# The last item's products with W1-W2 by a seven-product scheme, with partial sums chained in one PSUM tile, and a new list of steps

## The chip, the cores and the metric

The kernel runs on one core of a Trainium2 chip. The metric is device time in microseconds (us) of one launch. In the profile, PE is TensorE's matmul, PEld its weight load, DVE is VectorE, ACT is ScalarE, POOL is GpSimd and SP is SyncE.

## The reference, cut to what matters

There are four batch items (B = 4), each with 8 heads, 768 positions and head size 64. A block-sorting attention gives each item a matrix X of 768 tokens by 512 channels. Then a feed-forward part follows:

```
h1 = x @ w1                 # 512 -> 1024
h2 = x @ w2                 # 512 -> 1024
out = maximum(h1, h2) @ w_out   # 1024 -> 512
```

The kernel uses that maximum(h1, h2) = h2 + relu(h1 - h2). So it forms D = W1 - W2 once, computes g = relu(X D), and then out = g W_out + X Wc with Wc = W2 W_out, which is also formed once. Inputs are loaded as bf16; PSUM and the outputs are fp32.

## The kernel before, in words

All of the kernel is one hand-written list of steps, the string `plan`. A step is a word such as `h3.0.1A`: a kind, its indices, and an engine letter at the end (A for ACT, D for DVE, P for POOL) that says who reads the result out of PSUM or does the sum. `token` calls one function for each word, and each engine executes its instructions in the order in which the words stand. PSUM is one pool of four tiles of two banks each (`psum`, tag "ps"), so at most four results wait for their readers at a time.

The front of the list prepares everything: `k`, `q`, `b` and `t` sort and turn K, Q and V, `s` and `v` are scores and values of the attention, `x` transposes its result into `xT`, `T` transposes W2 into `w2T`, `d` subtracts W2 from W1 in place (`w_difference`, after which `w1_sb` holds D), `c` forms Wc, `w` forms sums of weight blocks. The words `lk`, `lq`, `lf`, `lv` issue loads on POOL's queue. Item 0's work is mixed into this front; the items then overlap, and the last item (3) ends the list.

For each item, a step `h<item>.<ch>.<t>` (`moe_h`, line 719) computes g for one half `ch` of the tokens (384) and one of four pieces `t` of 256 features: eight matmuls of 384 columns at line 711 and one reader (ACT, line 725, or DVE, line 727). An item has eight such steps.

The output product of an item is done in two groups, `P` (token tiles 0 and 1 of each half) and `U` (tile 2), by `Group`. A group has seven steps, `P3.0` to `P3.6`, by a Strassen scheme: matrices are cut into 2 by 2 blocks, and seven block products with sums of blocks take the place of eight. The sums of X's blocks are `X` steps (`x_sums`, into `sums_x`), those of g's blocks `G` steps (`g_sums`), those of weights `w` steps. A product of `P` is 12 matmuls of 256 columns, one of `U` is 6 (line 839). Each product is read out of PSUM by a copy or an add (lines 865, 872, 874), and the add's other input is an earlier result in SBUF. The finished halves are stored by `store`, from SP's queue and, for the very last part, from ACT's.

After the item's transposes, the end of the list before is the eight `h3` steps, and then the fourteen steps of `P3` and `U3`, mixed with X and G sums.

Of the kernel before, what the change touches and what calls it, by code (L numbers as in the profile page):

```python
# [10 lines left out]
FP32 = mybir.dt.float32  # L11
BF16 = mybir.dt.bfloat16
# [4 lines left out]
def kernel(  # L17
# [16 lines left out]
    nc = tc.nc  # L34
# [16 lines left out]
    TCH = S // 2  # L51
# [15 lines left out]
    def ps_f32(name):  # L67
        return psum.tile([128, 1024], FP32, tag="ps", name=name)
# [663 lines left out]

    sums_g = big.tile([128, 3, 4, TCH], BF16, tag="sums_g", name="sums_g")
    sums_x = big.tile([128, 4, 2, TCH], BF16, tag="sums_x", name="sums_x")
    wt_early = big.tile([128, 2, 4, NW], BF16, tag="wt_early", name="wt_early")
    w2T_flat = w2T.rearrange("p f d -> p (f d)")
    wt_late = w2T_flat[:, 0 : 8 * NW].rearrange("p (n k f) -> p n k f", n=2, k=4)
# [72 lines left out]
    class Group:  # L810
# [66 lines left out]
        def store(self, ch, c0=0, c1=DMODEL, queue=nc.sync):  # L877
# [5 lines left out]
                in_=self.o[ch][:, :, c0:c1],  # L883
            )

        def step(self, at, eng):
            a = self.by_tile(self.a) if at else None
            if at == 0:
                n = len(self.tiles)
                self.ps = ps_f32("out_ps")  # L890
                self.a = opool.tile([128, self.w], FP32, tag=f"a{n}", name="a", bufs=1)
                if n == 1:
                    o = opool.tile([128, 2, DMODEL], FP32, tag="o1", name="o", bufs=1)
                    self.o = [o[:, ch : ch + 1] for ch in range(2)]
                    self.both = o
                else:
                    self.o = [
                        opool.tile([128, n, DMODEL], FP32, tag=f"o{n}", name="o", bufs=2)
                        for _ in range(2)
                    ]  # L900
                self.product(0, "a11", "b11", True)
                self.first = self.copy(self.by_tile(self.a), 0, eng)
            elif at == 1:
                self.product(1, 2, 2, True)
                self.second = self.add(1, 0, 1, a, [self.first], eng)
            elif at == 2:
                self.product(0, "a12", "b21", False)
                self.copy(self.part(0, 0), 0, eng)
            elif at == 3:
                self.product(1, 1, 1, False)  # L910
                self.third = self.add(0, 1, 1, a, [self.first], eng)
            elif at == 4:
                self.product(0, 3, 3, True)
                self.fourth = self.add(1, 1, 0, self.part(0, 1), [self.third], eng)
                if self.b == B - 1:
                    self.store(1, NW)
            elif at == 5:
                self.product(1, 4, "b22", False)
                self.fifth = self.add(0, 1, 1, a, [self.first, self.fourth], eng)
                if len(self.tiles) > 1 or self.b == B - 1:  # L920
                    self.store(0)
            else:
                self.product(0, "a22", 4, False)
                self.add(
                    1, 0, 0, self.part(1, 0), [self.first, self.second, self.fifth], eng, True
                )
                if self.b == B - 1:
                    self.store(1, 0, NW, nc.scalar)
                elif len(self.tiles) > 1:
# [44 lines left out]
    def token(text):  # L974
# [6 lines left out]
        if kind == "k":  # L981
            sort_k(*n, eng=eng)
        elif kind == "q":
            q_transposes(*n, eng)
        elif kind == "F":
            fills[0] = n[0] * 128
        elif kind == "s":
            scores(*n, fills.pop(0, 0))
        elif kind == "v":
            values(*n, fills.pop(0, 0))  # L990
        elif kind == "x":
            x_transposes(*n, eng)
        elif kind == "t":
            turn_v(slice(0, 128), eng, n[1] * 24, n[1] * 24 + 24)
        elif kind == "b":
            {0: sort_v, 2: sort_v_pair, 3: sort_v_halved}[n[0]](*n, eng=eng)
        elif kind == "p":
            pair_q(*n, eng)
        elif kind == "y":
            nc.gpsimd.tensor_copy(  # L1000
                out=landed.rearrange("p (c h n) -> p c h n", c=2, n=1),
                in_=xT[:, n[0] % 2, :, :, 0, 0:1],
            )
            nc.gpsimd.tensor_copy(out=landed[:, 0:2], in_=qT[n[0] + 1][:, 0:HP:2, 0, 0])
        elif kind == "lv":
            load_v(3, half=n[0])
        elif kind == "lk":
            load_k(n[0])
        elif kind == "lq":
            load_q(n[0])  # L1010
        elif kind == "w":
            weight_sums(*n, engine)
        elif kind == "c":
            w_product(n[0], eng)
        elif kind == "X":
            x_sums(*n, engine)
        elif kind == "G":
            g_sums(*n, engine)
        elif kind == "h":
            moe_h(*n, eng=eng)  # L1020
        elif kind == "ha":
# [17 lines left out]
    groups, fills = {}, {}  # L1039
    landed = const.tile([128, 4], BF16, tag="landed", name="landed")  # L1040
    plan = [
        """
        k0.1A d0P k0.2A b0.1A b0.3D q0.0D b0.0D b0.2A q0.1D s0.5 s0.4 v0.5 s0.6 T0D s0.7 v0.4
        s0.0 v0.6 s0.1 s0.2 v0.7 s0.3 x0.2D v0.2 x0.3A lk1 lq1 v0.1 ha0.1.0 v0.0 hb0.1.0A T3D
        T2A lf3 d1P x0.0A v0.3 ha0.1.1 lf2 d3D lf1 hb0.1.1A B0 T1A ha0.0.1 d2D x0.1A X0.1D
        ha0.1.3 lf0 hb0.1.3A ha0.0.0 ha0.0.2 hb0.0.2D ha0.1.2 hb0.0.0D w0.3D c3D X0.2D G0.1.1D
        w0.1D hb0.1.2A hb0.0.1D G0.0.1D k1.1D lq2 c0A G0.1.2D c2A X0.3D k1.2D G0.1.3D k1.0A
        X0.4D q1.0D G0.0.2D q1.1A c1D s1.1 t1.2D s1.6 w1.1D t1.3D ha0.0.3 w1.2D w0.2D t1.1D
        t1.0D hb0.0.3A lk2 s1.3 s1.7 w1.4D lk3 P0.0A G0.0.4D s1.2 w0.4D s1.4 P0.1D b2.3A G0.0.3D
        b2.1A p2.0D p2.1D G0.1.4D P0.2A w1.3D b2.6D b2.4A b2.0A P0.3D b2.5A b2.2D b2.7A q2.0  # L1050
        P0.4D v1.1 v1.7 s1.5 q2.1 P0.5D v1.4 v1.6 P0.6D x1.3 k2.2A s1.0 U0.0A v1.5 U0.1D v1.2
        x1.2 v1.0 U0.2A k2.1A v1.3 U0.3D k3.2D k2.0A U0.4D U0.5D x1.0 x1.1 s2.7 s2.5 s2.6 U0.6D
        h1.1.0A v2.5 h1.1.3A X1.1D v2.7 X1.2D X1.4D k3.1A k3.0A h1.1.1A s2.4 s2.0 G1.1.1D
        h1.0.1A G1.1.2D X1.3D h1.0.3A v2.6 v2.0 h1.1.2D y1 h1.0.0A G1.0.1D G1.1.3D h1.0.2A lq3
        G1.0.3D G1.0.2D p3.0D P1.0D p3.1A q3.0 G1.1.4D s2.2 q3.1 lv0 G1.0.4D s2.3 lv1 s2.1 x2.3
        P1.1D P1.2A v2.2 U1.0D v2.3 P1.3D v2.1 U1.1D v2.4 P1.4D t3.1D x2.2 x2.1 U1.2A U1.3D s3.4
        t3.3D t3.0D s3.5 P1.5D x2.0 s3.2 s3.3 t3.2D P1.6D U1.4D b3.0D b3.1A s3.7 U1.5D U1.6D
        b3.3D b3.2A s3.0 h2.1.1A v3.7 h2.1.3A h2.1.2D v3.0 v3.5 G2.1.1D h2.1.0A h2.0.1A G2.0.1D
        v3.4 X2.3D h2.0.0A h2.0.3A U2.0A G2.1.2D s3.6 X2.1D X2.2D G2.0.2D G2.1.3D s3.1 h2.0.2A
        P2.0D v3.1 x3.2 x3.0 U2.1D G2.0.3D G2.0.4D v3.3 P2.1D P2.2A v3.6 U2.2A G2.1.4D v3.2  # L1060
        U2.3D x3.3 U2.4D X2.4D P2.3D P2.4D U2.5D x3.1 P2.5D U2.6D P2.6D h3.0.0A h3.1.0D h3.1.1A
        h3.1.2A G3.0.1D X3.1D h3.0.1A h3.1.3A U3.0A h3.0.3A G3.0.2D G3.1.1D G3.1.2D G3.0.3D
        X3.3D X3.2D h3.0.2D P3.0A G3.0.4D U3.1D P3.1D G3.1.3D P3.2A U3.2D G3.1.4D P3.3D X3.4D
        U3.3D P3.4D P3.5D P3.6D U3.4D U3.5D U3.6D
        """,
    ]
    for part in plan:
# [30 lines left out]
```

## Time and profile before

| what | value |
|---|---|
| median of 3 runs | 162.32 us (161.71 to 162.54) |
| profiled execution: its time / its span | 161.68 us / 159.8 us |
| PE busy | 152.5 us (95%), 2268 matmuls |
| DVE busy | 119.2 us (75%) |
| ACT busy | 82.6 us (52%) |
| POOL busy | 29.2 us (18%) |
| chain that ended last | PE 78%, DVE 10%, ACT 6% |
| of it, `out_ps` L839 / `h_ps` L711 | 31% / 26% |

The profile shows one execution; its time is 1.88 us above its span, which is what lies around the first and last instruction. A busy PE is one whose matmuls follow each other or overlap in the model of their ends, so the share alone doesn't tell how much is waiting; the table of waits and the start times do.

### The profile page before, as it was taken

The page shows a single profiled execution, that of the slowest core. Times are in us where ns is not written, and L with a number is a line of the kernel's source. Part 1 is how long each engine was busy: PE and PEld are TensorE (multiplying, and loading weights), DVE is VectorE, ACT ScalarE, POOL GpSimd, SP SyncE. Part 2 cuts the span into 40 slices and gives each one's busy share as a digit, 9 for nine tenths or more (in the row PEclk, how much of TensorE's full clock was granted, in tenths as well). Part 3 has the DMA queues.
Part 4 walks back from the last instruction along what each step waited for, and adds up shares of the span by engine and source line. Part 5 has one row for each costly group of instructions (what it writes and reads, how often), then busy time and mean ns, then how long its engine had stood idle before and what let it go on. Part 6 is the DMA issues. An engine that isn't in the chain of part 4 may idle for free.

```text
span 159.8 us, 5180 instructions
## 1 busy us (share of the span) xinstructions
PE 152.5 (95%) x2268; PEld 117.2 (73%) x2272; DVE 119.2 (75%) x262; ACT 82.6 (52%) x107; POOL 29.2 (18%) x57
## 2 busy tenths in 40 slices
PE   6999799999999989999999999999999999999990
PEld 7958678655566878886766898866679885678880
DVE  4875899949899998794659699966939854385661
ACT  3489896922269982457874904673561002642000
POOL 7949997130010000001600000000000000000000
PEclk9999999999999999999999999999999999999999
DMA  3999999999999998795899894760202409000055
GB/s 39 203 207 197 168 193 204 213 222 215 209 202 218 216 201 86 264 138 149 138 217 215 166 150 109 219 235 0 53 1 53 99 34 360 4 0 0 0 202 196
DMA packets 28918, 23.93 MB, mean 150 GB/s; under 512 B 16672, under 2 KB 24608, under 8 KB 28896
## 3 DMA queue, kind: packets, MB, share of 16 engines
q0 software_dynamic: 9280, 13.37, 47.8%
q1 hardware_dynamic: 19200, 9.84, 25.8%
q8 instruction: 18, 0.29, 0.8%
q10 hardware_dynamic: 416, 0.39, 0.7%
q14 instruction: 4, 0.03, 0.1%
HBM read 26.75 MB, written 6.29 MB: 207 GB/s over the span
## 4 chain that ended last, share of the span: by engine, by line
PE 78%; DVE 10%; ACT 6%; issue 2%; DMA 1%; DVEq 0%
PE out_ps L839 31%; PE h_ps L711 26%; PE o_ps L609 5%; PE wc_ps L691 4%; PE k_ps L486 4%; PE s_ps L581 3%; ACT e L597 2%; ACT kT L109 2%; ACT v_sb L109 2%; DVE w2T L757 1%; DMA p_sb<-in_sort_net_dram 1%; DVE v_dc L252 1%; PE tq_ps L453 1%; PE tx_ps L647 1%; PE tw_ps L672 1%
## 5 line engine op out<-in xcount | busy, mean ns | idle before, releaser
L711 PE MATMUL h_ps<-xT,w_sb 128*128 128x384 bf16 x256 | 44.8, 326 | 0.0
L725 ACT ACTIVATE g<-h_ps 128x768 bf16<-128x768 f32 x25 | 20.3, 811 | 28.4 <-PE h_ps L711 28.4
L711 PEld LDWEIGHTS <-w_sb 128*128 128x128 bf16 x256 | 23.9, 98 | 14.8
L597 ACT ACTIVATE e<-s_ps 96x768 bf16<-96x768 f32 x32 | 24.1, 807 | 4.0 <-PE s_ps L581 3.8
L626 DVE TENSOR_TENSOR x<-o_ps,rs 96x512 bf16<-96x512 f32 x32 | 22.0, 686 | 1.1
L839 PEld LDWEIGHTS <-g 128*128 128x128 bf16 x192 | 18.1, 98 | 2.4
L865 DVE TENSOR_TENSOR o<-out_ps,a 128x512 f32<-128x512 f32 (+1 forms) x24 | 13.2, 551 | 4.1 <-PE out_ps L839 4.0
L839 PEld LDWEIGHTS <-sums_g 128*128 128x128 bf16 x144 | 13.7, 98 | 1.7
L839 PE MATMUL out_ps<-wo_sb,g 128*128 128x256 bf16 x96 | 13.1, 273 | 0.0
L609 PE MATMUL o_ps<-v_sb,e 96*128 96x65 bf16 x256 | 12.3, 193 | 0.7 <-ACT e L597 0.5
L609 PEld LDWEIGHTS <-e 96*128 96x128 bf16 x256 | 10.9, 98 | 2.6 <-ACT e L597 0.7
L865 DVE TENSOR_TENSOR o<-out_ps,o 128x512 f32<-128x512 f32 (+1 forms) x16 | 8.9, 556 | 5.0 <-PE out_ps L839 3.8
L839 PE MATMUL out_ps<-w2T,sums_x 128*128 128x256 bf16 x72 | 11.8, 273 | 0.0
L109 ACT CAST kT<-k_ps 128x1024 bf16<-128x1024 f32 x9 | 8.8, 1015 | 5.0 <-PE k_ps L486 5.0
L109 ACT CAST v_sb<-v_ps 96x1024 bf16<-96x1024 f32 x10 | 9.8, 1016 | 3.0 <-PE v_ps L528 1.7
L727 DVE TENSOR_SCALAR g<-h_ps 128x768 bf16<-128x768 f32 x7 | 6.7, 953 | 5.8 <-PE h_ps L711 5.8
L874 ACT COPY o<-out_ps 128x512 f32<-128x512 f32 (+1 forms) x7 | 3.5, 496 | 13.7 <-PE out_ps L839 13.7
L620 DVE RECIPROCAL rs<-o_ps 96x8 f32<-96x8 f32 x32 | 6.3, 196 | 4.7 <-PE o_ps L609 4.7
L839 PEld LDWEIGHTS <-sums_x 128*128 128x128 bf16 x96 | 8.7, 98 | 1.1
L581 PE MATMUL s_ps<-qT,kT 64*128 64x96 bf16 x256 | 9.1, 204 | 0.4 <-ACT e L597 0.2
L83 PE MATMUL fill_ps<-fill 128*128 128x118 bf16 x92 | 7.6, 271 | 1.2 <-DVE fill L74 1.2
L581 PEld LDWEIGHTS <-kT 64*128 64x128 bf16 x256 | 6.2, 94 | 3.4 <-issue 1.7
(122 smaller groups left out, 239.2 us busy)
## 6 DMA issues: line engine op xcount, KB each, us to landing
out_dram<-o SPq DMA_DIRECT2D x10, 512.0 KB, 3.5
v_raw<-in_v_dram POOLq DMA_DIRECT2D x8, 384.0 KB, 15.8
k_raw<-in_k_dram POOLq DMA_DIRECT2D x3, 768.0 KB, 14.6
w_sb<-in_moe_w_dram POOLq DMA_DIRECT2D x4, 256.0 KB, 5.8
w_sb<-in_moe_w_dram POOLq DMA_DIRECT2D x2, 512.0 KB, 9.2
wo_sb<-in_moe_w_out_dram POOLq DMA_DIRECT2D x2, 512.0 KB, 12.8
v_raw<-in_v_dram POOLq DMA_DIRECT2D x3, 256.0 KB, 5.0
k_raw<-in_k_dram POOLq DMA_DIRECT2D x3, 256.0 KB, 6.6
```

Of the source, the lines that this page charges most:

```text
L83: nc.tensor.matmul(ps[:, 0:w], w0, fill[:, 0:w], start=True, stop=True)
L109: nc.scalar.copy(out=out_ap, in_=in_ap)
L486: nc.tensor.matmul(ps[r0 : r0 + 64, m * 64 : (m + 1) * 64], kv[r0 : r0 + 64, t * 16 + m, :], bd_k[b][r0 : r0 + 64, :], start=True, stop=True,)
L581: nc.tensor.matmul(ps[:, h2 * 512 + ii * 128 : h2 * 512 + ii * 128 + BLK], kT[b][rows, (hp * 8 + i) * BLK : (hp * 8 + i) * BLK + 128], rhs ...
L597: nc.scalar.activation(out=e_out, in_=src, func=AF.Exp, scale=scale)
L609: nc.tensor.matmul(ps[:, h2 * 512 + ii * 65 : h2 * 512 + (ii + 1) * 65], e[:, (h2 * 4 + ii) * BLK : (h2 * 4 + ii) * BLK + 128], v_sb[:, m0 ...
L626: nc.vector.tensor_tensor(out=x, in0=ov[:, :, :, 0:D], in1=rs.to_broadcast([BLK, 2, 4, D]), op=ALU.mult,)
L711: nc.tensor.matmul(h_ps[ch, t][:, m * 512 : m * 512 + TCH], w1_sb[:, hp, fb * 128 : (fb + 1) * 128], xT[:, b % 2, ch, hp % 2, hp // 2, :], ...
L725: nc.scalar.activation(out=g, in_=src, func=AF.Relu)
L727: nc.vector.tensor_scalar(out=g, in0=src, scalar1=0.0, scalar2=None, op0=ALU.max)
L839: ins = nc.tensor.matmul(self.ps[:, bank * 512 + p * NW : bank * 512 + (p + 1) * NW], left(self.b, lw, k, ti * 128), right(rw, k), start=n ...
L865: ins = nc.vector.tensor_tensor(out=self.part(ch, half), in0=self.by_tile(self.bank(n)), in1=other, op=ALU.add)
```

## The change

Only the last item's feed-forward is computed in another way, and the list of steps is replaced by another one.

1. The eight steps `h3.*` go. In their place stand fourteen steps `Y3.<t>.<at>` (class `HGroup`): for each half `t` of the feature pieces, seven block products of X and D. A product is 4 matmuls of 384 columns. Four of the seven (0, 2, 3, 4) are accumulated one after another in one PSUM tile (`hb_ps`); after each of the first three the running sum is copied out as fp32 by ACT, and the next product is added on top in PSUM. Products 5 and 6 are accumulated in the same way in a second tile (`hq_ps`), which held product 1 before. The four parts of g come out of the readers: one directly by relu, three by a DVE add of PSUM and a kept copy, followed by a relu in place in SBUF, on ACT or DVE.
2. Four steps `Z1` to `Z4` (`d_sums`) form sums of D's blocks into `w2_sb`, 128 x 1024 bf16 each, on DVE.
3. For item 3, `Group.step` goes to `chain`: the same seven output products, but chained in bank 0 (products 0, 2, 3, 4) and bank 1 (1, then 5 and 6), with copies where adds of SBUF results were.
4. The list is new from the first word to the last; for items 0 to 2 it holds the same steps as before (and the Z sums), in another order. Of the steps that stand in both lists, 39 have their reader on another engine than before.

```diff
+    def d_sums(which, eng):
+        b11, b12, b21, b22 = d_blocks()
+        in0, in1 = {
+            1: (b12, b11),
+            2: (b22, d_turned(1)),
+            3: (b22, b12),
+            4: (b21, d_turned(2)),
+        }[which]
+        eng.tensor_tensor(out=d_turned(which), in0=in0, in1=in1, op=ALU.subtract)
...
+        def product(self, ps, lw, rw, new):
...
+            for m in range(2):
+                c = (2 * self.t + m) * 128
+                for k in range(2):
+                    nc.tensor.matmul(
+                        ps[:, m * 512 : m * 512 + TCH],
+                        w[:, k, c : c + 128],
+                        x[:, k],
+                        start=new and k == 0,
+                        stop=k == 1,
...
+        def result(self, ch, half, src, other, eng="D"):
+            g = gpool.tile([128, 2, TCH], BF16, tag="g", name="g")
+            if other is not None:
+                nc.vector.tensor_tensor(out=g, in0=src, in1=other, op=ALU.add)
+                if eng == "A":
+                    nc.scalar.activation(out=g, in_=g, func=AF.Relu)
+                else:
+                    nc.vector.tensor_scalar(
+                        out=g, in0=g, scalar1=0.0, scalar2=None, op0=ALU.max
+                    )
...
+        def step(self, at, eng):
+            if at == 0:
+                self.p = ps_f32("hb_ps")
+                self.keep(self.first, self.product(self.p, (0, 0), (0, 0), True), eng)
+            elif at == 1:
+                self.q = ps_f32("hq_ps")
+                src = self.product(self.q, (0, 1), (1, 0), True)
+                self.result(0, 0, src, self.first, eng)
+            elif at == 2:
+                self.keep(self.own[:, 0], self.product(self.p, 2, 2, False), eng)
+            elif at == 3:
+                self.keep(self.own[:, 1], self.product(self.p, 1, 1, False), eng)
+            elif at == 4:
+                self.result(0, 1, self.product(self.p, 4, (1, 1), False), None, eng)
+            elif at == 5:
+                self.result(1, 1, self.product(self.q, 3, 3, True), self.own[:, 1], eng)
+            else:
+                self.result(1, 0, self.product(self.q, (1, 1), 4, False), self.own[:, 0], eng)
...
         def step(self, at, eng):
+            if at and self.b == B - 1:
+                self.chain(at, eng)
+                return
```

The front of the list, before and after (its first two lines), and the end after:

```diff
-        k0.1A d0P k0.2A b0.1A b0.3D q0.0D b0.0D b0.2A q0.1D s0.5 s0.4 v0.5 s0.6 T0D s0.7 v0.4
-        s0.0 v0.6 s0.1 s0.2 v0.7 s0.3 x0.2D v0.2 x0.3A lk1 lq1 v0.1 ha0.1.0 v0.0 hb0.1.0A T3D
+        k0.1D k0.2A b0.2A b0.0D b0.3A q0.0D q0.1D s0.4 b0.1D s0.5 s0.6 s0.7 lk1 v0.4 s0.0 v0.6
+        s0.3 v0.5 d0P s0.1 T1D s0.2 d1P v0.7 x0.2A v0.1 T0A x0.3D ha0.1.0 v0.0 ha0.1.1 v0.2
...
+        P2.2A x3.2 U2.3D v3.1 Z3D P2.3D G2.0.4D x3.0 P2.4D U2.4D U2.5D P2.5D P2.6D U2.6D X3.1D
+        X3.2D X3.3D Y3.1.0A Y3.0.0A Y3.1.1D Y3.1.2A Y3.0.2A X3.4D Y3.0.1D Y3.1.3A Y3.0.3A
+        Y3.0.5A Y3.1.5D Y3.1.4A Y3.0.4A Y3.0.6A Y3.1.6A G3.0.1D G3.0.2D G3.1.1D G3.1.2D P3.0A
+        U3.0D P3.1D P3.2A G3.1.4D G3.0.3D G3.0.4D U3.1D U3.2A G3.1.3D P3.3D P3.5D U3.3A P3.4A
+        P3.6D U3.5D U3.4D U3.6D
```

More of the change, by code (lines that the diff above doesn't have):

```diff
@@ L734, with d_blocks, d_turned @@
     sums_x = big.tile([128, 4, 2, TCH], BF16, tag="sums_x", name="sums_x")
+    def d_blocks():
+        return [
+            w1_sb[:, 2 * half : 2 * half + 2, f * DFF // 2 : (f + 1) * DFF // 2]
+            for half in range(2)
+            for f in range(2)
+        ]
+    def d_turned(n):
+        return w2_sb.rearrange("p t f -> p (t f)").rearrange(
+            "p (n k f) -> p n k f", n=4, k=2
+        )[:, n - 1]
+    def d_sums(which, eng):
[7 more added lines that the diff above has]
+        eng.tensor_tensor(out=d_turned(which), in0=in0, in1=in1, op=ALU.subtract)
@@ L884, in store, with chain @@
             )
+        def chain(self, at, eng):
+            if at == 1:
+                self.product(1, "a12", "b21", True)
+                self.add(0, 0, 1, self.by_tile(self.a), [self.first], eng)
+            elif at == 2:
+                self.product(0, 2, 2, False)
+                self.second = self.copy(self.part(1, 0), 0, eng)
+            elif at == 3:
+                self.product(0, 1, 1, False)
+                self.third = self.copy(self.part(1, 1), 0, eng)
+            elif at == 4:
+                self.product(0, 4, "b22", False)
+                self.copy(self.part(0, 1), 0, eng)
+                self.store(0)
+            elif at == 5:
+                self.product(1, 3, 3, True)
+                self.add(1, 1, 1, self.part(1, 1), [self.third], eng)
+                self.store(1, NW)
+            else:
+                self.product(1, "a22", 4, False)
+                self.add(1, 0, 1, self.part(1, 0), [self.second], eng)
+                self.store(1, 0, NW, nc.scalar)
         def step(self, at, eng):
+            if at and self.b == B - 1:
+                self.chain(at, eng)
+                return
             a = self.by_tile(self.a) if at else None
@@ L914, in step @@
                 self.fourth = self.add(1, 1, 0, self.part(0, 1), [self.third], eng)
-                if self.b == B - 1:
-                    self.store(1, NW)
             elif at == 5:
@@ L926, in step @@
                 )
-                if self.b == B - 1:
-                    self.store(1, 0, NW, nc.scalar)
-                elif len(self.tiles) > 1:
+                if len(self.tiles) > 1:
                     self.store(1)
@@ L1020, in token @@
             moe_h(*n, eng=eng)
+        elif kind == "Y":
+            if (n[0], n[1]) not in h_groups:
+                h_groups[n[0], n[1]] = HGroup(n[0], n[1])
+            h_groups[n[0], n[1]].step(n[2], eng)
+        elif kind == "Z":
+            d_sums(n[0], engine)
         elif kind == "ha":
@@ L1037, in token @@
             groups[key].step(n[1], eng)
-    groups, fills = {}, {}
+    groups, h_groups, fills = {}, {}, {}
     landed = const.tile([128, 4], BF16, tag="landed", name="landed")
@@ L1049 @@
[L1049 to L1060, printed above, removed]
@@ new lines @@
+        hb0.1.1A lq1 v0.3 lf1 hb0.1.0A x0.0D T3D d3D T2A d2D x0.1A ha0.0.1 ha0.0.0 ha0.1.3
+        hb0.1.3A X0.1D X0.2D hb0.0.1A ha0.1.2 hb0.0.0A B0 ha0.0.2 hb0.1.2A w0.3D G0.0.1D w0.1D
+        hb0.0.2A c0A G0.0.2D X0.4D k1.0D k1.1A lf3 lf2 k1.2D X0.3D G0.1.1D c3D G0.1.2D c2D q1.0A
+        q1.1D c1A s1.4 w0.2D w1.1D lf0 G0.1.3D G0.0.3D s1.1 s1.2 ha0.0.3 hb0.0.3A t1.3D t1.2D
+        w1.2D P0.0A s1.3 t1.1D t1.0D s1.7 s1.6 G0.0.4D w0.4D P0.1D b2.1A G0.1.4D lq2 lk2 b2.3A
+        P0.2A p2.0D w1.3D b2.2D p2.1D b2.4A w1.4D b2.7A P0.3D q2.0 q2.1 b2.5A b2.6D b2.0A P0.4D
```

47 lines of the change are left out of this document (38 added, 9 removed).

## The prediction

> **What bounds the kernel now.** I read the page first: how busy each engine is, and the granted clock.
>
> ```profile
> PE 152.5 (95%) x2268; PEld 117.2 (73%) x2272; DVE 119.2 (75%) x262; ACT 82.6 (52%) x107; POOL 29.2 (18%) x57
> ...
> PEclk9999999999999999999999999999999999999999
> ```
>
> PE is busy nearly throughout and its clock is full in every slice. The share alone can hide waits, so I asked next for PE's waits.
>
> ```profile
> PE fill_ps L83 <- DVE fill L74: 1.2, 1, 1.2
> PE v_ps L551 <- DVE v_sb L111: 0.6, 1, 0.6
> PE o_ps L609 <- ACT e L597: 0.5, 1, 0.5
> PE v_ps L507 <- ACT v_sb L109: 0.3, 1, 0.3
> PE s_ps L581 <- ACT e L597: 0.2, 1, 0.2
> ```
>
> Columns are total us, times, longest. The first is the start. The others come to 1.6 us; by the timeline they lie at 16.7, 19.3, 23.1 and 57.8 us. After 58 us PE waits for nobody. Then the end of the chain that ended last:
>
> ```profile
> 123.91 7.86 PE out_ps L839 x72
> 131.77 7.80 PE h_ps L711 x48
> 139.57 0.65 PE out_ps L839 x6
> 140.22 2.60 PE h_ps L711 x16
> 142.82 13.13 PE out_ps L839 x120
> 155.98 0.42 DVE o L865
> ```
>
> Columns are start, length, what. The last item is pure PE work: 64 matmuls of line 711 in 10.40 us, 162.5 ns each, and 126 of line 839 in 13.78 us, 109.4 ns each; then one DVE add and the last store, to 159.8. So the end moves by what PE's work in this stage changes, unless a reader becomes late. What readers cost is in the groups kept apart by shape:
>
> ```profile
> L725 ACT ACTIVATE g<-h_ps 128x768 bf16<-128x768 f32 x25 | 20.3, 811 | 28.4 <-PE h_ps L711 28.4
> ...
> L865 DVE TENSOR_TENSOR o<-out_ps,a 128x512 f32<-128x512 f32 x12 | 8.2, 687 | 3.3 <-PE out_ps L839 3.1
> ...
> L727 DVE TENSOR_SCALAR g<-h_ps 128x768 bf16<-128x768 f32 x7 | 6.7, 953 | 5.8 <-PE h_ps L711 5.8
> ...
> L785 DVE TENSOR_TENSOR sums_g<-g 128x768 bf16<-128x768 bf16 x8 | 4.3, 553 | 5.0 <-ACT g L725 5.0
> ...
> L874 ACT COPY o<-out_ps 128x512 f32<-128x512 f32 x4 | 2.4, 588 | 7.3 <-PE out_ps L839 7.3
> ...
> L414 DVE COPY q_pair<-w_sb 128x1536 bf16<-128x1536 bf16 x2 | 1.0, 556 | 0.0
> ```
>
> **The change: PE's work.** Eight h steps of 8 matmuls become fourteen Y steps of 4: 64 matmuls become 56, same shape, same weight size. 8 x 162.5 ns = 1.30 us less. The output products keep their 126 matmuls.
>
> **Readers in the last stage.** Before, eight readers (six ACT, two DVE). After: six ACT copies of 768 fp32 columns, six DVE adds, two relus out of PSUM, six relus in place. Copies: 811 ns for 768 columns into bf16, 588 ns for 512 into fp32 (and 586 for 512 into bf16, so the output type costs nothing): I take 0.81 us, 1.02 (the 1024-column casts of line 109) as upper bound. Adds: 687 ns for 512, and a relu of 768 is 953: 0.95 us. The relu in place has no row: on ACT 0.80 (the 768-column xT copy, 801 ns); on DVE at most 0.56 (a 1536-column bf16 copy) and not under 0.28, half of that; I take 0.35, since the columns are half as many and some part is fixed. Three of them are ACT's, three DVE's. In sum ACT has 8 x 0.81 + 3 x 0.80 = 8.9 us, DVE 6 x 0.95 + 3 x 0.35 + 4 X sums of 0.55 = 9.0 us, beside 9.10 us of PE: three engines nearly level. So order decides, and I laid the three orders against each other. Time 0 is where PE ends `U2.6`; data are readable 0.20 us after PE's last slot of a product (the overhang of 0.16 of a matmul of 326 ns and 0.04 to start the reader), and PE goes on 0.05 us after a reader.
>
> - `Y3.1.0` 0 to 0.65, `Y3.0.0` to 1.30, `Y3.1.1` to 1.95. ACT's copies: 0.85 to 1.66 and to 2.47. DVE: U2.6's add, X3.1, X3.2 to 1.72.
> - `Y3.1.2` adds onto the first copy's tile: free at 1.71, X3.2 at 1.77, PE there at 1.95. `Y3.0.2`: free at 2.52, PE at 2.60. `Y3.0.1` at 3.25 needs only a fresh tile.
> - ACT copies these at 2.80 to 3.61 and to 4.42. `Y3.1.3`: free 3.66, PE 3.90. `Y3.0.3`: free 4.47, PE 4.55. ACT copies to 5.56 and 6.37.
> - `Y3.0.5` overwrites the tile that DVE reads for `Y3.0.1` until 5.09 (X3.3, the add and relu of `Y3.1.1`, X3.4 stand ahead of it): 5.14 against 5.20. `Y3.1.5` at 5.85, `Y3.1.4` at 6.50, `Y3.0.4` at 7.15 are free early.
> - `Y3.0.6`: DVE's add of `Y3.0.5` waits for ACT's copy at 6.37 and ends at 7.38; PE at 7.80. `Y3.1.6`: 8.39 against 8.45. PE is through at 9.10.
> - `P3.0` needs a tile: `Y3.1.4`'s relu ends at 9.03. Then `U3.0`, `P3.1` to 12.38 cover what is still behind: relus on ACT to 11.4, four G sums on DVE to 12.9. `P3.2` reads X sums first and g's second half only at 13.26.
> - In P3 and U3 each chained product has one to two others between it and the copy that it waits for (1.3 to 2 us against 0.20 + 0.59 + 0.05); only `U3.6`, behind `U3.5`'s add and DVE's backlog, is about 0.05 late.
>
> So PE should wait hardly at all, but with covers of 0.02 to 0.4 us. The stage gives 1.30 - 0.05 = 1.25 us. With copies at 1.02 us, `Y3.0.2` is 0.35 late and later links add about 0.1: 0.80 us. The tail (add, store) is unchanged.
>
> **Z sums.** Four DVE ops of 128x1024 bf16, 684 ns by the rows of line 757, 2.7 us in all. They stand where DVE has room: `Z1` with `P1.0`, `Z2` and `Z4` among the h2 steps, `Z3` behind `v3.1`. Behind them in DVE's queue stand readers of `X1.4`, `v2.5`, `P1.1`; I get `P1.1` read at 17.6 us after the start of item 1's h steps, where `P1.3`, its waiter, stands at 18.3. Cost 0; without cover 0.7 each. The operands are safe: `w2_sb` holds item 2's q until `p2.1`, long before.
>
> **The new list for items 0 to 2.** Between 58 us and the last item PE never waits, and it does the same work, so this can only lose there. The narrowest places: `b3.0` needs the last `t3` on DVE, which is busy without a break for 27 us ahead of it by my layout (about 1 us of cover by start-to-start spacings); `x3.0` is issued about 1.2 us after `v3.1` and lands in 2.8 us (median of the transposes), with 7.2 us of PE work between `v3.1` and the Y steps. SP's later stores are behind it, not ahead. Before 58 us there is 1.6 us of waiting to win. Walked in the same way from 12.3 us on: `k0.1` on DVE ends K two thirds of a us earlier, so the eight exps begin at 17.9 instead of 18.5, but `b0.1` on DVE holds `v0.4` until 19.8 (19.3 before, with two score steps fewer done); `ha0.0.1` ends 0.3 us earlier for equal work. Up to `P0.1` DVE has some 1 us less queued (readers moved to ACT), and I find its add at 53.4 instead of 53.8. On POOL the k load now passes both `d` subtractions and the q load falls behind them: issued 25.0 instead of 22.6; the loads are busy back to back up to 60 us, so its landing (17.6 us after issue before, 40.2) hardly moves, and `q1.0` stands at 43.5. I take 0.2 us of gain, bounds 1.6 gain and 1.5 loss.
>
> **Sum.** The profiled execution, 161.68 us, would be 161.68 - 1.25 - 0.20 = 160.2. The median lies 0.64 above that execution, so 162.32 - 1.45 = 160.9 us. A change of 0.5%, 0.8 us, is about what a measurement of this kernel can tell from none.
>
> **Rivals.** *The chain's waits take the gain back.* A chained link is 0.65 + 0.20 + 0.81 + 0.05 = 1.71 us long, and two chains alternating give PE only 1.30 us per link; only the product-1, 5 and 6 steps between fill the rest. If the fillers are not ready when their turn comes, each of the three links shows 0.41 us: 1.23 us, time 162.1. For it: covers of 0.06; against: the rows are steady and the walk closes. The Trainium skill, "Perfetto Trace Analysis", section "Matmuls", asks that independent matmul groups rotate through different PSUM banks so that one's evacuation overlaps the next group's matmuls; the chain gives that up within a half. By that rule the result is this rival, 162.1, not 160.9; no row of this trace bears it out or refutes it, since P and U share their two banks among several products already and PE doesn't wait there.
>
> *Slower, by the front.* T1 now comes before T0 and as early as about 21.4 us. It reads the second quarter of W2, issued at about 15.0. PE's order is strict, so a late quarter stops everything. `d0P` started at 19.97 on the first quarter of W1 without waiting, and 256 KB more at 200 GB/s is 1.3 us: 21.3, just in time. But the slowest of these loads took 10.0 us to land; then T1 starts at 25.0, 3.6 late, of which 0.8 would be waiting for exps anyway: 2.8 lost, 160.9 + 2.8 = 163.7. It decides from a landing at 23.6 on (1.45 lost beyond the 0.8).
>
> *More from the front.* If all 1.6 us of waits vanish: 162.32 - 1.25 - 1.6 = 159.5.
>
> *It doesn't save.* The matmul count leaves no doubt about 8 fewer; that PE's rate is lower in 4-matmul pieces has no row for it: the `U` products of 6 run at the same 109 ns as those of 12.
>
> **Numbers.** Forecast 0.56 (160.2 to 161.5); chain's waits 0.19 (same, 161.5 to 162.7); front slower 0.13; front better 0.12. So faster 0.68, same 0.19, slower 0.13. Range 159.7 to 162.7: from most of the better front to the chain's waits, leaving out the slow front and its opposite end.
>
> **What would show it.** Matmuls of the Y line: 56, 162.5 ns apart, in about 9.1 us, and from the first Y step to PE's last matmul 22.9 us where it was 24.2. ACT copies of 768 columns at 0.81, DVE adds at 0.95. PE waits on ACT or DVE from the Y steps on under 0.3 in sum. PE waits ahead of 58 us near 1.4. Wrong would be: gaps of 0.1 to 0.4 at each chained link, a wait of PE's weight load for W2 at line 672, or a DVE wait that holds a `P` or `b` step between 60 and 130 us.

## The result, and the profile after

The changed kernel takes 159.75 us (median of 6 runs, 159.41 to 160.55) beside 162.12 us (6 runs, 161.71 to 162.54) of the kernel before: ratio 0.9856, 95% interval 0.9825 to 0.9886. The forecast was 160.9 us with a range of 159.7 to 162.7, so the result lies 1.1 us below the forecast and just above the range's lower end. The profiled execution took 159.69 us, its span is 157.9 us (before: 161.68 and 159.8).

The page after, busy time and granted clock:

```profile
PE 149.7 (95%) x2260; PEld 115.1 (73%) x2264; DVE 127.1 (81%) x274; ACT 84.4 (53%) x111; POOL 29.3 (19%) x57
...
PEclk9999999999999999999999999999999999999999
```

PE has 8 matmuls fewer, as counted; DVE has 12 instructions and 7.9 us more. The clock is full as before. PE's waits after (total us, times, longest):

```profile
PE fill_ps L83 <- DVE fill L74: 1.2, 1, 1.2
PE fill_ps L83 <- DVE rowsum L273: 0.5, 1, 0.5
PE s_ps L581 <- issue: 0.4, 1, 0.4
PE tq_ps L433 <- DMA q_raw<-in_q_dram: 0.4, 1, 0.4
PE tw_ps L672 <- DVE rs L620: 0.2, 1, 0.2
PE pe L358 <- DVE p_bf L280: 0.2, 1, 0.2
```

By the timeline all lie ahead of 22 us. The wait for `v_sb` at L551 (0.56 us at 57.8 before) is gone. T1's wait at L672 is 0.23 us, for a PSUM tile whose reader on DVE is late, not for W2. There is no wait at all from the first Y step on, and the chain that ended last shows the same (start, length, what):

```profile
123.31 7.21 PE out_ps L934 x66
130.51 1.30 PE hb_ps L779 x8
131.81 0.65 PE hq_ps L779 x4
132.46 1.30 PE hb_ps L779 x8
133.76 0.65 PE hq_ps L779 x4
134.41 1.30 PE hb_ps L779 x8
135.71 1.30 PE hq_ps L779 x8
137.01 1.30 PE hb_ps L779 x8
138.31 1.30 PE hq_ps L779 x8
139.61 13.86 PE out_ps L934 x126
153.47 0.02 issue
153.50 0.42 DVE o L960
```

Every row begins where the one above it ends: 56 matmuls in 9.10 us, then 126 without a break. From the start of the last stage's first matmul to that of its last group the timeline gives 23.74 us before (131.60 to 155.34) and 22.51 after (130.35 to 152.86): 1.23 us less. The readers, from the groups kept apart by shape:

```profile
L798 DVE TENSOR_TENSOR g<-hq_ps,hs 128x768 bf16<-128x768 f32 x4 | 3.6, 953 | 0.9 <-ACT hs L791 0.8 <-PE hq_ps L779 0.2
L791 ACT COPY hs<-hb_ps 128x768 f32<-128x768 f32 x4 | 3.0, 802 | 0.9 <-PE hb_ps L779 0.9
L800 ACT ACTIVATE g<-g 128x768 bf16<-128x768 bf16 x3 | 2.5, 843 | 1.2 <-DVE g L798 1.0
...
L802 DVE TENSOR_SCALAR g<-g 128x768 bf16<-128x768 bf16 x3 | 1.1, 360 | 0.1
```

**Where the time went, by the two traces.** From the front's first matmul at line 358 (11.49 us before, 11.16 after) to the first matmul of the last stage: 120.11 and 119.19 us, 0.92 less. The last stage: 1.23 less. From PE's last group to the span's end: 4.46 us before and 5.04 after, 0.58 *more*. With the 0.33 us by which the front starts earlier (it scatters between 11.12 and 11.51 over all kernels here) this is the 1.9 us between the spans. So there are two questions behind the result: what gained 0.9 in the front, where 0.2 had been taken, and what lost 0.6 behind the last matmul, where the forecast had taken no change.

### The profile page after: what moved, and what is told of

The parts are those of the page before. It is cut to its first block, busy times and chain, and to the rows that moved or that the text cites. A ratio compares the mean times of both kernels' runs of the same rounds, so it can differ in the third digit from the quotient of the medians.

```text
span 157.9 us, 5185 instructions
## 1 busy us (share of the span) xinstructions
PE 149.7 (95%) x2260; PEld 115.1 (73%) x2264; DVE 127.1 (81%) x274; ACT 84.4 (53%) x111; POOL 29.3 (19%) x57
## 4 chain that ended last, share of the span: by engine, by line
PE 80%; DMA 9%; DVE 6%; issue 1%; POOL 0%; ACT 0%; DVEq 0%; POOLq 0%
PE out_ps L934 33%; PE h_ps L711 20%; DMA q_raw<-in_q_dram 6%; PE wc_ps L691 4%; PE o_ps L609 4%; DMA v_raw<-in_v_dram 3%; PE hb_ps L779 3%; DVE x L626 3%; PE s_ps L581 3%; PE hq_ps L779 2%; PE k_ps L486 2%; PE v_ps L551 2%; PE tw_ps L672 1%; PE tq_ps L453 1%; DVE o L960 1%
## 5 line engine op out<-in xcount | busy, mean ns | idle before, releaser
L711 PE MATMUL h_ps<-xT,w_sb 128*128 128x384 bf16 x192 | 33.9, 326 | 0.1
L711 PEld LDWEIGHTS <-w_sb 128*128 128x128 bf16 x192 | 17.8, 98 | 10.8
L725 ACT ACTIVATE g<-h_ps 128x768 bf16<-128x768 f32 x20 | 16.0, 812 | 15.1 <-PE h_ps L711 14.9
L960 DVE TENSOR_TENSOR o<-out_ps,a 128x512 f32<-128x512 f32 (+1 forms) x20 | 11.0, 550 | 3.4 <-PE out_ps L934 2.1
L109 ACT CAST kT<-k_ps 128x1024 bf16<-128x1024 f32 x7 | 7.0, 1013 | 3.4 <-PE k_ps L486 3.4
L111 DVE CAST v_sb<-v_ps 96x1024 bf16<-96x1024 f32 x6 | 7.3, 1216 | 1.2 <-PE v_ps L528 0.8
L779 PEld LDWEIGHTS <-w_sb 128*128 128x128 bf16 x56 | 5.5, 98 | 3.5
```

The costliest lines, as they stand in the source:

```text
L109: nc.scalar.copy(out=out_ap, in_=in_ap)
L111: nc.vector.tensor_copy(out=out_ap, in_=in_ap)
L711: nc.tensor.matmul(h_ps[ch, t][:, m * 512 : m * 512 + TCH], w1_sb[:, hp, fb * 128 : (fb + 1) * 128], xT[:, b % 2, ch, hp % 2, hp // 2, :], ...
L725: nc.scalar.activation(out=g, in_=src, func=AF.Relu)
L779: nc.tensor.matmul(ps[:, m * 512 : m * 512 + TCH], w[:, k, c : c + 128], x[:, k], start=new and k == 0, stop=k == 1, skip_group_check=True,)
L960: ins = nc.vector.tensor_tensor(out=self.part(ch, half), in0=self.by_tile(self.bank(n)), in1=other, op=ALU.add)
```

## The experiments

Each kernel was run beside the kernel before, whose median was 162.0 to 162.1 us each time.

**e1: the list alone.** The new list for items 0 to 2, the old last item.

```diff
-        (the new words from X3.1D on, and Z1 to Z4)
+        h3.0.0A h3.1.0D h3.1.1A ... U3.6D   (the last item's words of the list before)
```

> The new list for items 0 to 2 (without the Z sums) with the old last item: eight h3 steps, the old output groups and the old end of the list. Theory A (two parts that add: the last item saves 1.23 us of PE work between its first product and PE's end, the list saves the rest by fewer PE waits ahead of 58 us): the last stage takes 24.2 us again from its first matmul to PE's last, it begins about 1.2 us earlier than before's 131.6, and the time is about 161.0, ratio to before 0.993. Rival B (the list was made for the new last item and gains nothing by itself; what looks like its gain is scatter of the start and of single executions): time equal to before, ratio 0.997 to 1.003.

160.79 us, ratio 0.9932 (0.9906 to 0.9957). The front, measured as above, takes 119.16 us; the wait at 57.8 is gone, as it is in all eleven profiles of kernels with the new list.

**e2: the last item alone.** The old list for items 0 to 2, with the four Z sums put in, and the new last item.

```diff
+        X1.4D Z1D ... h2.0.1A Z2D ... h2.0.0A Z4D ... h2.0.2A Z3D
```

> The old list for items 0 to 2 with the four Z sums put where VectorE has room, and the new last item with the new end of the list. Theory A: the last stage takes 22.95 us, it begins at 131.6 as before, time about 160.9, ratio 0.9925. Rival B: the last item carries the whole gain, ratio 0.986. Rival C (the Z sums have no cover in the old list): up to 4 times 0.65 us lost, ratio 0.993 to 1.008.

160.86 us, ratio 0.9925 (0.9908 to 0.9942). The old wait is there:

```profile
PE v_ps L551 <- DVE v_sb L111: 0.6, 1, 0.6
```

The two parts add up: 0.0068 + 0.0075 = 0.0143, measured together 0.0144. So the list is worth about 1.1 us and the last item about 1.2.

**e5: one letter of the old list.** Why does the wait at 57.8 go?

```diff
-        w0.3D c3D ... c1D s1.1
+        w0.3D c3D ... c1A s1.1
```

> The kernel before with one letter of its list changed: c1, the copy of the first selection block's product (about 1 us of VectorE's queue ahead of 58 us), goes to ScalarE. Theory A: the new list gained 0.57 us of its 0.98 because TensorE's wait of 0.56 us at 57.8 (v_ps at L551, released by VectorE's v_sb) was a backlog on VectorE. Then the wait is gone or under 0.2 here, and the time falls by 0.4 to 0.6: 161.5 us, ratio 0.997. Theory B: the wait is made by something that the two lists order otherwise (the step v0 itself stands too near to its reader). Then the wait stays at 0.4 to 0.6 and the time at 162.05, ratio 1.000.

161.14 us (12 runs), ratio 0.9959 (0.9940 to 0.9978), which is 0.66 us of gain. The timeline of PE, of the kernel before and of this one (start, length; a wait stands in brackets at the end):

```profile
57.83 0.88 PE L551 MATMUL v_ps<-bd,v_dc 64*128 64x64 bf16 x48 [0.56 <-DVE v_sb L111]
```

```profile
57.87 0.89 PE L551 MATMUL v_ps<-bd,v_dc 64*128 64x64 bf16 x48
```

The wait is missing in this profile, but PE starts no earlier than before. This execution was the slowest of the twelve (162.34 us; its span is 159.9, the others' 159.0 to 159.7). PE lost 0.64 us in it in two pauses for which the profile names no releaser, and VectorE's cast comes at the same time in both kernels (before, then e5):

```profile
56.56 1.22 DVE L111 CAST v_sb<-v_ps 96x1024 bf16<-96x1024 f32 x1
```

```profile
26.85 0.84 PE L672 MATMUL tw_ps<-ident,w_sb 128*128 128x128 bf16 x12 [0.37 <-issue]
45.16 1.10 PE L453 MATMUL tq_ps<-ident,q_raw 64*64 64x64 bf16 x57 [0.27 <-issue]
56.60 1.21 DVE L111 CAST v_sb<-v_ps 96x1024 bf16<-96x1024 f32 x1
```

So the missing wait alone shows nothing here: PE came late. What the trace does show is that VectorE is less behind PE. The add of `P0.1` starts 0.70 us behind the end of its product in the kernel before (53.06 to 53.76) and 0.10 us behind it in e5 (53.68 to 53.78). The times exclude theory B, which expected no gain; the gain is somewhat above theory A's 0.4 to 0.6, which lies inside the interval. That VectorE's backlog made the wait is thus supported by the runs, though no trace shows PE reaching this place earlier. The new list has `c1A` too.

**e3: without the output chain.** The new Y steps and list, but `P3` and `U3` in the old order of products and with the old stores (`Group.step` without `chain`).

> As the changed kernel up to the last Y step, but item 3's output products in the old order with adds of results in SBUF. Its second product needs the second g and X sums at once, where the chained order has a product of plain blocks there. Theory A: the order matters by its wait alone; the last of the four G sums ended 12.7 us after the first Y product, and PE would get to that sum 11.95 us after it, so PE waits 0.8 us and the time is about 160.5, ratio 0.991. Rival: the chained copies and the adds cost alike and the sums come early enough, time 159.75, ratio 0.9856.

159.76 us, ratio 0.9864 (0.9829 to 0.9899). The stage is as I expected, the time is not. PE waits once,

```profile
PE out_ps L934 <- DVE sums_g L880: 0.5, 1, 0.5
```

at 143.19 us, and the stage takes 23.30 instead of 22.51 us: 0.79 more. By the start times PE is held twice, 0.2 us at 142.13 and 0.6 us at 143.19, each time until 0.05 us behind the end of a G sum on DVE. But behind the last add it is 1.2 us quicker: 2.74 us from the add's end to the span's end, where the changed kernel needs 3.98. So the order of the output products is worth 0.8 us to PE here, since its second product reads no G sum, and something at the end takes more than that back: the profiled span is 157.5 us, 0.4 less than the changed kernel's. The runs' times don't tell the two kernels apart (158.98 to 160.94 us here).

**e4: the halves in turn.** All seven `Y3.1` steps, then all seven `Y3.0` steps, so that at most one other product lies between a chained one and the copy that it waits for.

```diff
-        Y3.1.0A Y3.0.0A Y3.1.1D Y3.1.2A Y3.0.2A X3.4D Y3.0.1D Y3.1.3A Y3.0.3A Y3.0.5A ...
+        Y3.1.0A Y3.1.1D Y3.1.2A X3.4D Y3.1.3A Y3.1.5D Y3.1.4A Y3.1.6A Y3.0.0A Y3.0.1D ...
```

> As the changed kernel, but all seven Y products of one half of the features before the other seven, so that a chained product stands one product or none behind the copy that it waits for. Theory A (a link of product, start of the copy, copy and return is 1.71 us, and only the other half's products hide it): by the same layout PE ends the Y steps 13.5 us after the first instead of 9.1, the wait per half lies at the chained steps 2, 3, 4 and 6, and the time is about 164, ratio 1.012. Rival (the copies are not what limits, PE's queue gets ahead anyway): 9.1 us and no change against the changed kernel.

166.88 us, ratio 1.0301 (1.0273 to 1.0328); the Y steps take 15.87 us. PE's waits, and then windows of 2 us (columns: start and end, length; PE, weight loads, DVE, ACT, POOL busy; granted clock; DMA share; GB/s):

```profile
PE hb_ps L779 <- ACT hs L791: 2.0, 3, 0.9
PE hb_ps L779 <- ACT ha L791: 1.4, 1, 1.4
```

```profile
132.00:134.00 2.00, 0.81 (x4) 0.42 (x5) 1.97 (x5) 0.94 (x2) 0.00 (x0) 1.00 1.05 405
...
138.00:140.00 2.00, 0.82 (x6) 0.39 (x4) 0.51 (x1) 1.39 (x2) 0.00 (x0) 1.00 0.00 0
140.00:142.00 2.00, 0.93 (x5) 0.49 (x5) 1.32 (x2) 0.93 (x2) 0.00 (x0) 0.98 0.00 0
142.00:144.00 2.00, 2.00 (x7) 0.88 (x6) 0.00 (x0) 0.65 (x1) 0.00 (x0) 0.50 0.00 0
144.00:146.00 2.00, 1.96 (x8) 0.88 (x7) 0.96 (x1) 0.46 (x2) 0.00 (x0) 0.67 0.04 8
```

The first half takes 6.86 us, about half of the 13.5 that I had expected, but the second takes 9.0, so the Y steps and the time (164 expected) came out longer. The chained links do show their waits once at most one product lies between. Beyond that the clock fell to 0.50 after 4 us in which PE was busy 0.82 and 0.93 of 2 us; behind the one window of 0.81, at 132 to 134, it did not fall. The longest single gap is 1.37 us. The Trainium skill, "TensorE: Matmul & The Clock Gate", section "A second HAM failure mode: psum-queue depth-cycling", says that PE idling briefly but often between groups makes the clock go back and forth between half and full. This trace agrees in so far as the clock fell once, to 0.50, and came back; a repeated change is not seen.

**e8: the same, with one copy on VectorE.** The 1.4 us wait was for a copy that stood behind a relu on ScalarE.

```diff
-        Y3.1.4A Y3.1.6A Y3.0.0A Y3.0.1D
+        Y3.1.4A Y3.1.6A Y3.0.0D Y3.0.1D
```

> The variant that runs all Y steps of one half before those of the other (166.88 us, Y steps in 15.87 us, granted clock down to 0.50 at 142 to 144 us), with one letter changed: the second half's first copy goes to VectorE, so it no longer stands behind ScalarE's relu of the first half. Theory A: the clock fell because the waits at the turn, 1.4 us for that copy among them, took TensorE's busy share down to 0.8 to 0.9 of each 2 us; without it the clock stays at 0.95 or more and both halves take about 6.8 us: Y steps 13.7 us, time 164.2, ratio 1.013. Theory B: the four waits of 0.9 us and less for copies that remain are enough for the clock to fall: Y steps 14.5 to 15.5 us, granted clock 0.5 to 0.7 in two windows of 2 us, time 165.5 to 166.5, ratio 1.024.

164.12 us, ratio 1.0125 (1.0090 to 1.0160). The Y steps take 13.97 us (130.18 to 144.15), and the same windows show a full clock although waits for copies remain:

```profile
PE hb_ps L779 <- ACT hs L791: 2.2, 4, 0.9
...
PE hb_ps L779 <- DVE ha L793: 0.6, 1, 0.6
```

```profile
138.00:140.00 2.00, 1.31 (x8) 0.58 (x6) 1.90 (x3) 0.88 (x2) 0.00 (x0) 1.00 0.00 0
140.00:142.00 2.00, 1.19 (x8) 0.73 (x8) 0.48 (x2) 1.10 (x2) 0.00 (x0) 1.00 0.00 0
142.00:144.00 2.00, 1.58 (x10) 0.73 (x9) 0.96 (x1) 0.98 (x2) 0.00 (x0) 1.00 0.03 8
```

Theory A holds: one letter brings 2.8 us (166.88 to 164.12) of the 7.1 that e4 loses against the changed kernel, and the clock stays full. Not all of the 2.8 is the copy's wait and the clock: PE's last stage takes 29.85 us in e4, 27.57 in e8 and 22.51 in the changed kernel, so by the profiles 2.3 us lie there, and 0.7 us in the stretch behind the last add (3.41 and 2.69 us), which has another cause (see e11). What the stage still loses in e8, 5.1 us, comes with the order of one half after the other.

**e6 and e7: which part of the output chain costs the end?** e6 chains only `P3`, e7 only `U3`; the other group goes the old way, with its old stores and the old order of its words.

```diff
-            if at and self.b == B - 1:
+            if at and self.b == B - 1 and len(self.tiles) > 1:     # e6; "== 1" in e7
                 self.chain(at, eng)
```

> The changed kernel, but of the last item's output products only the two-tile group P is chained; the one-tile group U goes by the old order with its old stores. After the last add the changed kernel needed 3.98 us to the span's end, the one without the output chain 2.74, the kernel before 3.4; in the first, one DMA engine works alone for about 1.1 us at the end. Theory A: that trailing engine belongs to U's chained ending. Then the end of the span is 2.7 to 3.4 us behind the last add here, TensorE's stage stays near 23.1 us, and the span is 157.0 to 157.4 (changed kernel 157.9), the time 159.2, ratio 0.982. Theory B: it belongs to P's early stores. Then 3.9 to 4.0 us, span 157.9 to 158.1, time 159.9, ratio 0.986. Theory C, scatter: anything between, and the companion run goes the same way.

> The companion: only the one-tile group U of the last item's output products is chained; P goes by the old order with its old stores. TensorE's stage from the first Y matmul to its last should come out between 22.95 (both chained) and 23.74 (none), taken as 23.5. Theory A (the trailing DMA engine belongs to U's chained ending): 3.9 to 4.0 us from the last add to the span's end, span 158.4, time 160.3, ratio 0.989. Theory B (to P's early stores): 2.7 to 3.4 us, span 157.3 to 157.9, time 159.5, ratio 0.984.

e6: 159.46 us, ratio 0.9858 (0.9823 to 0.9893), profiled span 157.2. e7: 160.43 us, ratio 0.9912 (0.9879 to 0.9944), span 158.4. Both spans are as theory A had them; e6's time is 0.3 above it. For PE it is clear: the stage takes 22.44 us in e6 and 23.28 in e7, so the whole gain of 0.8 belongs to `P3`'s order, and chaining `U3` gives PE nothing. For the end, 3.30 us behind the last add in e6 speak for A; 3.66 in e7 lie between A and B, so these two runs don't decide it.

**e9 and e10: the queues.** Two of `U3`'s stores are swapped, in e6 (e9) and in the changed kernel (e10, whose edit is shown).

```diff
-                self.store(0)
+                self.store(0, queue=nc.sync if len(self.tiles) > 1 else nc.scalar)
...
-                self.store(1, 0, NW, nc.scalar)
+                self.store(1, 0, NW, nc.scalar if len(self.tiles) > 1 else nc.sync)
```

> The variant that chains only P of the last item's output products (span 157.2 us, 3.3 us of it behind the last add), with two stores of U swapped between the queues: its 256 KB store goes to ScalarE's queue and the last one of 128 KB to SyncE's, so the two queues carry 1,024 and 512 KB instead of 1,152 and 384. Theory A: the single DMA engine that works on at the end belongs to the longer queue's backlog. Then the stretch behind the last add falls from 3.3 to 2.7 us, span 156.6, time 158.8, ratio 0.981. Theory B: it doesn't hang on the queues' shares. Then 3.3 to 3.4 us, span 157.2, time 159.4, ratio 0.985.

> The changed kernel (span 157.9 us, 3.98 us of it behind the last add) with the same two stores of U swapped between SyncE's and ScalarE's queues. Theory A: the stretch falls to 3.3 us, span 157.3, time 159.2, ratio 0.982. Theory B: 3.9 to 4.0 us, span 157.9, time 159.75, ratio 0.986.

e9: 159.01 us, ratio 0.9817 (0.9792 to 0.9843), span 157.3, of it 3.36 behind the last add. e10: 159.66 us, ratio 0.9859 (0.9836 to 0.9883), span 158.1, of it 3.82. By the spans theory B holds: the end does not hang on the queues' shares. The time of e9 alone would not have told, since it lies between the 158.8 and 159.4 of the two theories.

**e11 and e12: eight idle memsets.** In windows of half a us behind the last add the changed kernel shows the stores' end (columns as above):

```profile
155.00:155.50 0.50, 0.00 (x0) 0.00 (x0) 0.00 (x0) 0.00 (x0) 0.00 (x0) 1.00 0.50 172
155.50:156.00 0.50, 0.00 (x0) 0.00 (x0) 0.00 (x0) 0.00 (x0) 0.00 (x0) 1.00 0.07 25
156.00:156.50 0.50, 0.00 (x0) 0.00 (x0) 0.00 (x0) 0.00 (x0) 0.00 (x0) 1.00 0.07 25
```

A share of 0.07 is one of 16 DMA engines: one trails by a us. The DMA view has one thing on a single engine at that time. Its queues of instruction packets (packets, MB, share), first of the kernel before, then of the changed one:

```profile
q8 instruction: 18, 0.29, 0.8%
q14 instruction: 4, 0.03, 0.1%
```

```profile
q8 instruction: 17, 0.28, 0.7%
q14 instruction: 5, 0.04, 0.1%
```

The changed kernel has a fifth packet of q14, and windows of 0.2 us place it at 153.9 to 154.1, among the last stores. In the kernels with 271 VectorE instructions and more such a packet comes before the end; in the kernel before (262), e1 (265) and e5 (261) the next q14 packet behind 90 us comes only after the span's end. The Trainium skill, "Runtime: NRT & Kernel Launch", section "Instruction fetch mechanics", says that an engine's instruction memory is refilled in blocks of 16 KiB, the next one fetched while the current one is executed. The trace agrees for q8, whose packets are 0.28 MB / 17 = 16 KB; those of q14 are half of that, 0.04 MB / 5, and here the measurement decides. That the packet belongs to VectorE is inferred from these counts. If it does, eight more instructions on VectorE, far ahead, should bring it forward:

```diff
+                    if self.b == 0:
+                        pad = const.tile([128, 8], FP32, tag="pad", name="pad")
+                        for i in range(8):
+                            nc.vector.memset(pad[:, i : i + 1], 0.0)
```

> The changed kernel with eight memsets of 128x1 elements more on VectorE, behind the first item's last output add (about 72 us, where VectorE is idle 0.9 of 3 us). What they are for: in each trace the DMA view shows one instruction packet (queue q14, 8 KB, on a single DMA engine) among the last stores, and its place goes with the stretch from the last add's end to the span's end: 2.5 us ahead of the last add with 2.74 us (no output chain), 0.1 to 0.3 ahead with 3.3 and 3.4 (P alone chained), 0.3 to 0.5 behind with 3.8 to 4.0 (changed kernel and two more). The packet's place fits a count of VectorE's instructions, so eight more of them should bring it eight instructions forward, to about 145 us, ahead of the first store. Theory A: the engine that carries the packet late is the one that trails. Then the stretch falls to 2.7 to 3.4 us, span 157.2, time 159.1, ratio 0.982. Theory B: the packet moves, and the stretch stays at 3.8 to 4.0: span 157.9, time 159.75, ratio 0.986; the trailing engine has another cause.

> The best variant so far (P alone chained, two of U's stores swapped between the queues; span 157.2, time 159.01) with the same eight memsets. Theory A: the stretch behind the last add falls from 3.36 to about 2.75, as without the output chain, span 156.6, time 158.4, ratio 0.978. Theory B: span 157.2, time 159.0, ratio 0.982.

e11: 158.54 us (4 runs, 158.34 to 158.63), ratio 0.9780 (0.9764 to 0.9796), span 156.7. e12: 158.67 us, ratio 0.9811 (0.9781 to 0.9841), span 156.9. The DMA view of e11 has the packet where the expectation put it, at 144.4 to 144.6 us, and the windows of its end show no trailing engine:

```profile
154.50:155.00 0.50, 0.00 (x0) 0.00 (x0) 0.00 (x0) 0.00 (x0) 0.00 (x0) 1.00 0.98 365
155.00:155.50 0.50, 0.00 (x0) 0.00 (x0) 0.00 (x0) 0.00 (x0) 0.00 (x0) 0.85 0.56 197
```

By the DMA issues the last two stores land 2.2 and 1.9 us after their issue, where the changed kernel needs 3.4 and 3.0. A trailing engine is not new, either: the kernel before has one too, for a shorter time, behind a packet of q8 at 153.9 us:

```profile
158.00:158.50 0.50, 0.00 (x0) 0.00 (x0) 0.00 (x0) 0.00 (x0) 0.00 (x0) 1.00 0.07 25
```

All profiles side by side. The packet is the last q14 one, counted from the start of the last add. "Alone" is the last stretch in which at most two packets of the stores are under way at once, from the packet records of the traces. The end is from the end of the last add to the span's end:

| kernel | VectorE instructions | packet, us | alone, us | end, us |
|---|---|---|---|---|
| e11, e12 | 282, 283 | -8.9, -7.4 | 0.04, 0.03 | 2.87, 2.95 |
| e8 | 275 | -4.7 | 0.03 | 2.69 |
| e3 | 276 | -2.5 | 0.03 | 2.74 |
| e7 | 275 | -1.5 | 0.69 | 3.66 |
| e6, e9, e4 | 275, 275, 274 | -0.2, -0.2, -0.1 | 0.58, 0.60, 0.73 | 3.30, 3.36, 3.41 |
| e10, e2, changed | 274, 271, 274 | +0.3, +0.3, +0.5 | 1.16, 1.17, 1.28 | 3.82, 3.85, 3.98 |
| before, e1, e5 | 262, 265, 261 | none; a q8 packet at -2.0 to -2.1 | 0.66, 0.69, 0.75 | 3.40, 3.42, 3.47 |

Take the fourth column from the fifth, and 2.66 to 2.97 us are left in all fourteen: what differs between the ends is the time of one engine alone. It is nearly nothing in the four profiles whose packet starts 2.5 us or more ahead of the last add, and 0.6 to 1.3 us in the ten with a packet, of q14 or of q8, that starts later.

Theory A holds for the changed kernel: e11 is 1.2 us quicker, and its interval lies below that of the changed kernel. Its front (119.14 us) and its last stage (22.51) are as they were, so 1.11 us of this lie behind PE's last group. For e12 the trace goes the same way (from 3.36 us in e9 to 2.95), but the times don't decide: 158.67 beside 159.01 us, with intervals that overlap. What stays open is the size: the packet takes its engine only 0.31 us in the changed kernel, and the engine then works alone for 1.28. That the engine that trails is the one that carried the packet is an inference too, since the records don't name engines.

## Why the prediction was right or wrong, point by point

**PE's work and the stage: right.** 1.25 us were forecast, 1.23 measured; 9.10 us for the Y steps and 22.9 for the stage (22.51 and the last group's 0.44) came out as written. The readers' rows are right to 0.04 us: copies 0.80 (forecast 0.81), adds 0.95, the relu in place 0.36 on DVE (0.35) and 0.84 on ACT (0.80). The covers of 0.02 to 0.4 us held at every link. The order of the output products is part of this, and the prediction gave it no term. Kept in the old order (e3), the stage loses 0.79 us to two late G sums.

**Z sums: right.** They cost PE nothing in the new list: no wait stands between 58 us and the end. In e2, with another place for them, the front took 0.33 us longer than before, but that profile was the slowest of e2's six runs, and e5, which has no Z sums, shows the same 120.44 us, so this is not put down to them.

**The list: the step that was mis-sized.** "I take 0.2 us of gain, bounds 1.6 gain and 1.5 loss": e1 gives 1.1 us (0.7 to 1.5), the traces of the front 119.14 us (median of the eleven profiles with the new list) against 120.11, 0.97. The walk stopped at `P0.1`, where it had found less queued on DVE and the add 0.4 us earlier; it never asked whether that freed the wait of 0.56 us at 57.8, though it had that wait in its own table. In the changed kernel PE does get there earlier: the third piece of L551 starts 45.30 us behind the front's first matmul, where it was 46.34. e5's times put 0.66 us (0.36 to 0.97) down to one moved reader. The rest of the front's gain lies ahead of that wait, by the timelines: counted from the front's first matmul, PE reaches its first `c` product 0.93 us later than before (24.95 and 24.02 us), with 1.30 us more of item 0's work behind it, 0.37 us of gain, against the 0.2 that the walk took. The waits ahead of 58 us, forecast near 1.4 us, came to 1.1 behind the front's first matmul, 0.4 of it for a load of q.

**The tail: wrong.** "The tail (add, store) is unchanged": it grew by 0.58 us. The step that failed is that the stores' end was taken as the stores' own: in both kernels one DMA engine works alone at the end, 0.66 us before and 1.28 after, and this goes with the place of an instruction packet, which no view that I had read would have told. Without that stretch the two tails are 3.80 and 3.76 us.

**The number: in part luck.** By the traces the two terms that were wrong have opposite signs, 0.77 us too little gain in the front (0.20 taken, 0.97 found) and 0.58 us of loss at the end that had no term. They cancel in good part, and so the result stays inside the range, by 0.05 us; e11, which lacks the loss, lies outside it with 158.54. The sum also started from 162.32 us, the median of three runs, where six give 162.12. The account of the traces: 1.23 + 0.97 - 0.58 = 1.6 us are placed by the traces; the runs say 2.3 (1.9 to 2.8). The rest lies in the start (0.33) and in that the profile of before was 0.4 us quicker than its median and the profile after was at its median.

**The rivals.** *The chain's waits* (162.1): not in this order of steps. e4 and e8 show that the mechanism is real: with one other product between or none, chained links wait 0.2 to 0.9 us. The rule of the Trainium skill, "Perfetto Trace Analysis", section "Matmuls", on rotating through banks is met by two chains that take turns, so it didn't decide here: their fourteen products took 9.10 us without a wait, and 13.97 in e8, one half after the other at full clock. *Slower by the front* (163.7): T1 waited 0.23 us, and not for its load. *More from the front* (159.5): this is the side on which the result lies; 0.97 of its 1.6 us came. *It doesn't save*: refuted, 56 matmuls at 162.5 ns.

## What to carry to other kernels

In this kernel partial sums were chained in one PSUM tile at no cost, with two chains that alternate and at least two other products between a chained product and the next one on its tile. One chain after the other, the same instructions took PE 4.9 us more (13.97 for 9.10 us), and 6.8 where the clock fell too. A list that is walked for one edit has to be walked up to the next wait in the table, not up to the edit's own end. Where the last stores end a kernel, look in the DMA view for an instruction packet among them: here its place moved with the number of instructions on VectorE, and eight idle instructions far ahead of it were worth 1.2 us. And a wait that is missing in one profile shows a gain only if the engine also gets there earlier (e5).

## What the runs showed of the hardware that was not expected

The profile counts instruction packets on the same 16 DMA engines as the stores. In all fourteen profiles one engine worked alone for 0.6 to 1.3 us at the end when the last such packet started between 2.1 us ahead of the last add and 0.5 behind its start, and for at most 0.04 us when it started 2.5 us or more ahead; eight instructions that moved one packet were worth 1.2 us (e11). That the engine's part of the stores simply waits behind the packet is an inference, and a packet of 0.31 us is too small for all of it. The granted clock fell to 0.50 for some 3 us (142 to 145 us in e4) though no gap of PE was longer than 1.37 us: it fell behind two windows of 2 us with PE busy 0.82 and 0.93, and stayed at 1.00 behind a single one of 0.81 (e4) and behind 1.31 and 1.19 in a row (e8).
